# A tuned attention and gated feed-forward kernel: six tiles' x summed in PSUM, the flag inside the plan, another order at a chunk's end

## The chip, the cores and the metric

The kernel runs on one core of a Trainium2 chip. The metric is the device time of one execution in microseconds (us); for the kernel before it was taken three times, and a fourth execution was profiled. All rows and times below come from these runs. The engines are called as the profile calls them: PE (TensorE), DVE (VectorE), ACT (ScalarE), POOL (GpSimd) and SP (SyncE, which issues the transfers).

## The reference

```python
# attention: q, k, v are (4, 8, 768, 64), n_sink = 4, window = 128
scores = q @ k.transpose(0, 1, 3, 2) / sqrt(64)
keep = (pos_k < n_sink) | ((pos_q - pos_k >= 0) & (pos_q - pos_k < window))
a = softmax(where(keep, scores, -1e9))
x = (a @ v).transpose(0, 2, 1, 3).reshape(3072, 512)
# gated feed-forward on the 3072 tokens, d_model 512, d_ff 1536
out = (1 / (1 + exp(-(x @ w_gate))) * (x @ w_val)) @ w_out
```

Everything is fp32. The matrix products of the second part are made from split halves: each operand is a rounded "high" part and the rest as a "low" part, and a product is high x high + high x low + low x high.

## The kernel before, in words

**Attention.** A tile is 128 queries of one batch; tiles are worked in twelve pairs, heads by twos, so `attend` (L991) is called four times per pair of tiles, with a step number `u`. It makes the scores on PE (into the PSUM banks `a` or `o`), the masked exponential on DVE and ACT (`P`, `negm_all`, `sums`), turns P on PE (transposes `a<-ident,P`), copies it to `wt`, and multiplies it with v (`pv_one`, into a bank `a`); ACT copies that product into the SBUF buffer `xr` (256 columns for two heads). After the last heads of a pair `join` (L1260) adds the four sink keys: their probabilities `psk` are turned, copied to `sk`, multiplied with `vsp` into another bank, and DVE adds the bank to `xr`, 512 columns at a time. Then `copy` makes the high half `XH<-xr`, and `rest` the low half `XL<-xr,XH` (POOL or DVE).

There are four PSUM banks `a`, two `o` and two `m`. Scores, transposes, products with v and sink products share the banks `a`.

**Feed-forward.** Four of the twelve pairs (0, 1, 2 and 4) feed "direct" chunks while attention goes on: up products `m<-XH,wgh` and so on into the banks `m`, which DVE (`traw<-traw,m`) and ACT empty into `traw` and `graw`, and down products `o<-woh,graw`. The weights come in compressed and are decoded on the way (`w<-wst,zs`, then a high part `woh<-w` on ACT and its rest `wol<-w,woh` on DVE or POOL). The other eight pairs are stored to DRAM and come back later as four "wino" chunks: a Strassen-like form with seven products in place of eight (`passing` and `staying`, L2006 onward). A passing product has a rotating bank, which ACT or DVE adds to a sum `tf` in SBUF; three of the sums stay in banks `o` and `a`. At a chunk's end `merge` combines the sums with four additions and `emit` makes and stores four pieces of the output. In the kernel before all of that hangs behind the chunk's seventh product:

```python
fourth = coming.pop()
def done():
    fourth()
    merge(ci, sums)
    for n in range(4):
        emit(ci, g, n, O[n] if n < 3 else None, sums[n], False)
coming.append(done)
```

**The order.** No scheduler on the chip decides anything: a planner in Python (`Plan`) takes all operations with priorities, several possible engines and estimated lengths, and writes one fixed sequence per engine, with one helper line (L677 in the kernel before). Tables `RANKS` with hand-set numbers shift priorities of single operations. Where the planner sees PE without work in the first stretch it puts in filler matmuls `m<-ident` (`warm`), which compute nothing that is used.

**The end.** After the plan, DVE works out whether the inputs leave the fast path's limits (`bad`, five short instructions), PE sums that over the partitions (`a<-bad,one`), DVE makes `flag` and `total`, and every engine loads `total` and branches past the general path.

Of the kernel before, what the change touches and what calls it, by code (L numbers as in the profile page):

```python
# [9 lines left out]
F32 = mybir.dt.float32  # L10
# [12 lines left out]
NS = 4  # L23
# [8 lines left out]
RING = 6  # L32
# [47 lines left out]
SPLIT = 6  # L80
B_xr = 3
# [17 lines left out]
    A={0: 3.311, 10: -0.027, 200: 0.565, 400: -0.264, 600: -1.393, 635: 1.038, 665: -0.494, 695:  # L99
# [13 lines left out]
    G={0: 0.185, 200: -0.659, 400: -0.409, 600: 0.225, 635: -0.824, 665: 0.44, 695: -0.702, 725:  # L113
# [13 lines left out]
    M={0: -0.075, 2: -0.117, 3: -0.01, 4: 0.249, 5: -0.142, 6: -0.593, 7: -0.005, 8: 0.004, 9:  # L127
# [11 lines left out]
    P={0: 1.715, 200: 0.337, 400: -2.664, 600: 0.068, 1200: 0.132, 1500: -0.09, 1600: 2.607,  # L139
# [481 lines left out]
def kernel(  # L621
# [185 lines left out]
    for i in range(len(OS)):  # L807
        plan.over[f"o{i}", 0] = {("eO", i)}
# [1535 lines left out]
```

## Time and profile before

| what | us |
|---|---|
| runs | 714.39, 716.55, 717.35 |
| median | 716.55 |
| profiled execution, own time | 718.86 |
| its span, first to last instruction | 717.1 |
| mean granted TensorE clock (1 is full) | 0.996 |
| busy: PE / DVE / ACT / POOL | 700.7 / 570.0 / 381.4 / 522.2 |

The profiled execution is 718.86 − 716.55 = 2.31 us above the median of the runs, and 718.86 − 717.1 = 1.76 us of it lie outside the span. Busy time is a share of the span by engine; for PE the ends of matmuls are modelled. What an engine waits for in front of an instruction stands in brackets behind it, in us, with the releaser.

### The profile page before, as it was taken

The numbers are of one execution on the slowest core, as the hardware profiler recorded it, in microseconds if no ns is written. First come the engines' busy times: TensorE is split into PE (matmuls) and PEld (weight loads), VectorE is DVE, ScalarE is ACT, GpSimd is POOL, SyncE is SP. The second block draws the span as 40 slices with busy tenths as digits, with TensorE's granted clock in tenths as the row PEclk, the third lists the DMA queues.
The fourth block names the chain that finished last, engine by engine and source line by source line (L and its number), as shares of the span: only waits on it lengthen the run. The fifth ranks groups of instructions, "written<-read, shape, count | busy, mean of one in ns | idle before, by whom it ended". The sixth has DMA issues, their size and how long they took to land.

```text
span 717.1 us, 18023 instructions
## 1 busy us (share of the span) xinstructions
PE 700.7 (98%) x6488; PEld 649.7 (91%) x6488; DVE 570.0 (79%) x1296; ACT 381.4 (53%) x1052; POOL 522.2 (73%) x490
## 2 busy tenths in 40 slices
PE   8999899999999999999999999999899999999997
PEld 7778788888887888888999999999899999999996
DVE  8999989989895677875567798668888688886765
ACT  6898867754544565652453454543445444454431
POOL 3889867699997877764477697775768687786651
PEclk9999999999999999999999999999999999999999
DMA  9987879667776888855757656666467756665611
GB/s 291 295 245 257 289 235 311 233 211 251 245 246 193 273 264 264 283 143 173 233 178 227 185 163 202 210 220 186 154 182 216 227 184 176 184 206 183 187 50 64
DMA packets 110609, 152.75 MB, mean 213 GB/s; under 512 B 11060, under 2 KB 69428, under 8 KB 110516
## 3 DMA queue, kind: packets, MB, share of 16 engines
q1 hardware_dynamic: 110512, 151.56, 67.4%
q8 instruction: 52, 0.85, 0.5%
q14 instruction: 41, 0.34, 0.1%
q10 hardware_dynamic: 4, 0.00, 0.0%
HBM read 124.26 MB, written 27.26 MB: 211 GB/s over the span
## 4 chain that ended last, share of the span: by engine, by line
PE 77%; DVE 12%; DMA 4%; issue 3%; ACT 2%; POOL 1%; SPq 0%; DVEq 0%; POOLq 0%; ACTq 0%
PE a L677 38%; PE m L677 24%; PE o L677 15%; DVE tf L677 3%; DMA out_dram<-tf 2%; DVE w L677 2%; DVE a L677 1%; DVE tt L677 1%; DVE P L677 1%; DVE traw L677 1%; DMA wst<-in_moe_w_gate_dram 1%; DMA wst<-wol_d 1%; DVE XH L677 1%; DMA tf<-tw_d 1%; ACT P L677 1%
## 5 line engine op out<-in xcount | busy, mean ns | idle before, releaser
L677 POOL TENSOR_TENSOR tt<-tf,tt 128x512 fp32r<-128x512 f32 x75 | 103.3, 1389 | 26.9 <-ACT tt L677 11.6
L677 ACT ACTIVATE P<-P,negm_all 128x132 f32<-128x132 f32 x176 | 70.0, 399 | 23.7 <-DVE negm_all L677 23.4
L677 POOL TENSOR_SCALAR_AFFINE_SELECT wt<-wt 128x512 f32<-128x512 f32 (+1 forms) x88 | 63.1, 719 | 15.6 <-ACT wt L677 12.4
L677 PE MATMUL o<-woh,graw 128*128 128x512 f32 x192 | 74.1, 410 | 0.2 <-DVE graw L677 0.2
L677 ACT ACTIVATE tf<-a 128x512 f32<-128x512 f32 x49 | 29.3, 599 | 84.3 <-DVE a L677 62.3
L677 PE MATMUL m<-XH,wvh 128*128 128x256 f32 x216 | 61.6, 296 | 0.9 <-ACT traw L677 0.5
L677 ACT CAST tt<-tf 128x512 fp32r<-128x512 f32 x72 | 44.6, 620 | 27.9 <-PE a L677 21.8
L677 PE MATMUL m<-XH,wgh 128*128 128x256 f32 x193 | 56.5, 293 | 2.1 <-DVE traw L677 2.1
L677 PE MATMUL a<-xa,tt 128*128 128x256 f32 x360 | 57.2, 281 | 0.2 <-DVE a L677 0.2
L677 PE MATMUL m<-XH,wvl 128*128 128x256 f32 x204 | 57.4, 281 | 0.0
L677 PE MATMUL m<-XL,wvh 128*128 128x256 f32 x204 | 57.4, 281 | 0.0
L677 PE MATMUL m<-XH,wgl 128*128 128x256 f32 x192 | 54.4, 283 | 0.0
L677 PE MATMUL m<-XL,wgh 128*128 128x256 f32 x192 | 54.3, 283 | 0.0
L677 POOL TENSOR_TENSOR XH<-tf,XH 128x512 fp32r<-128x512 f32 x25 | 34.1, 1364 | 24.0 <-ACT XH L677 21.6
L677 PEld LDWEIGHTS a<-xa,tt 128*128 128x128 f32 x360 | 49.3, 188 | 0.5 <-DVE a L677 0.4
L677 POOL TENSOR_TENSOR XL<-tf,XL 128x512 fp32r<-128x512 f32 x14 | 18.2, 1303 | 41.2 <-ACT XL L677 41.2
L677 POOL TENSOR_TENSOR P<-P,rs 128x528 f32<-128x528 f32 x34 | 42.7, 1256 | 7.1 <-DVE rs L677 2.4
L677 PEld LDWEIGHTS m<-XH,wvh 128*128 128x128 f32 x216 | 40.0, 189 | 7.0 <-issue 2.9
L677 PEld LDWEIGHTS o<-woh,graw 128*128 128x128 f32 x192 | 36.1, 188 | 10.6 <-issue 3.7
L677 DVE TENSOR_TENSOR a<-a,big 128x256 f32<-128x256 f32 x72 | 30.4, 425 | 18.3 <-PE a L677 17.1
L677 PEld LDWEIGHTS m<-XH,wgh 128*128 128x128 f32 x193 | 36.7, 190 | 6.7 <-DVE traw L677 2.9
L677 DVE COPY_PREDICATED a<-tri,a 128x256 f32<-128x256 int32 (+1 forms) x90 | 30.7, 377 | 13.6 <-PE a L677 13.6
(409 smaller groups left out, 2647.1 us busy)
## 6 DMA issues: line engine op xcount, KB each, us to landing
tf<-tw_d SPq DMA_DIRECT2D x96, 256.0 KB, 3.2
wol<-wol_d SPq DMA_DIRECT2D x90, 256.0 KB, 3.5
qkT<-in_k_dram SPq DMA_DIRECT2D x30, 198.0 KB, 4.1
wgh<-tu_d SPq DMA_DIRECT2D x46, 128.0 KB, 2.7
wgl<-tu_d SPq DMA_DIRECT2D x46, 128.0 KB, 2.9
wvh<-tu_d SPq DMA_DIRECT2D x46, 128.0 KB, 2.6
wvl<-tu_d SPq DMA_DIRECT2D x46, 128.0 KB, 3.5
v<-in_v_dram SPq DMA_DIRECT2D x30, 192.0 KB, 3.6
```

The source lines that it names most:

```text
L677: return lambda *a, **kw: tc.keep_in_program_order(op(*a, **kw))
```

## The change

Four things change. First, for the first three pairs (`DIRECT = 3`; six tiles, the first twelve calls of `attend`) the products with v of the four head pairs write into two banks, each over 512 columns, and stay there; the sink products are added into the same banks, and the halves are made from there by the new function `straight`. The high half is made by ACT or DVE, the low half by DVE alone. Second, the flag's eight instructions are operations of the plan, at the end of attention. Third, the order of the seven products of the three wino chunks before the last is 0, 1, 2, 3, 5, 4, 6, and the pieces are stored as each is ready. Fourth, all numbers in `RANKS` are others (some 800; only their first line is shown), so that every engine's sequence is another one.

```diff
+DIRECT = 3
+HOLD = 1500.0
+OUTP = 0.5
...
-    A={0: 3.311, 10: -0.027, 200: 0.565, 400: -0.264, 600: -1.393, 635: 1.038, 665: -0.494, 695:
...
+    A={0: -0.166, 10: -8.671, 200: -1.192, 600: -1.977, 605: 0.724, 635: 1.407, 695: 0.285, 700:
...
+    for i in (1, 2):
+        plan.over["m2", i] = {("eM", 0)}
...
+        direct = n_of[b, t0] < DIRECT
         if h % 4 == 0:
-            XS.append(Tile(XR_, None, F32, "xr", 3))
+            if not direct:
+                XS.append(Tile(XR_, None, F32, "xr", 3))
+            elif u == 0:
+                XS.append(Tile(MS[1:], None, F32, "eM", 1))
+            else:
+                XS.append(Tile(AS, None, F32, "a", len(AS)))
...
         sides = [Tile(AS, None, F32, "a", len(AS)) for _ in range(2 - one)]
+        if direct:
+            assert one and T == 2 and not place[b, t0][0]
+            sides = [xst]
...
+        home = c * W if direct else 0
...
-                        sides[0]()[e * D : e * D + D, c0 : c0 + n], lhsT=vt()[:, e, l],
+                        sides[0]()[e * D : e * D + D, home + c0 : home + c0 + n], lhsT=vt()[:, e, l],
...
-                        start=i == 0, stop=i == len(wide) - 1, skip_group_check=True,
+                        start=i == 0 and not home, stop=i == len(wide) - 1, skip_group_check=True,
...
-            plan.op(
-                u, [("A", act(W, True), lambda: A.copy(out=xs()[:, c], in_=sides[0]()[:, 0:W]))],
-                [sides[0]], [(xst, c)],
-            )
+            if not direct:
+                plan.op(
+                    u, [("A", act(W, True), lambda: A.copy(out=xs()[:, c], in_=sides[0]()[:, 0:W]))],
+                    [sides[0]], [(xst, c)],
+                )
...
+    def straight(u, g, T, XS, sk, runs):
...
+        for i, acc in enumerate(XS):
+
+            def add(i=i, acc=acc):
+                for c in range(2):
+                    PE.matmul(
+                        acc()[:, c * W : c * W + W], lhsT=vs()[:, 2 * i + c], rhs=sk(),
+                        start=False, stop=True, skip_group_check=True,
+                    )
...
+            plan.op(
+                u, [
+                    ("A", act(2 * W, True), lambda x=x, hi=hi: A.copy(out=hi(), in_=x())),
+                    ("V", vec(2 * W), lambda x=x, hi=hi: V.tensor_copy(out=hi(), in_=x())),
+                ], [acc], [(XH, p) for p in parts],
+            )
+            rest(u, 2 * W, lo, x, hi, [acc] + [(XH, p) for p in parts], [(XL, p) for p in parts], True)
...
+        if n_of[b, t0] < DIRECT:
+            straight(u, g, T, XS, sk, runs)
+            return
...
-            fourth = coming.pop()
...
+            out_of = lambda n: lambda: emit(ci, g, n, O[n] if n < 3 else None, sums[n], False)
+            order = (0, 1, 2, 3, 5, 4, 6)
+            coming[:] = [coming[x] for x in order]
+            also(2, out_of(0))
+            also(4, lambda: merge(ci, sums), out_of(3))
+            also(5, out_of(2))
+            also(6, out_of(1))
...
+    plan.op(B * NT * H // 2 + 1.0, [("V", 900, odd_values)], [NEGM], [FLAG])
+    plan.op(B * NT * H // 2 + 1.0, [("PE", 200, counted)], [FLAG], [count])
+    plan.op(B * NT * H // 2 + 1.0, [("V", 400, decided)], [count], [FLAG])
```

The built programs count as follows, before and after: ACT copies `xr<-a` of 256 columns 48 and 36; DVE additions `xr<-a,xr` of 512 columns 22 and 18; the two `xr<-o,xr` are gone; `XH<-xr` on ACT 8 and 2, and three `XH<-a` and one `XH<-m` on ACT and two `XH<-a` on DVE are new; `XL<-xr,XH` on POOL 6 and 1, on DVE 2 and 1, and five `XL<-a,XH` and one `XL<-m,XH` on DVE are new. From the new numbers: fillers 50 and 45 (each is two matmul passes in the profile); `P<-P,rs` on POOL 34 and 25, on DVE 10 and 19; the rests of decoded weights on DVE 16 and 9, on POOL 20 and 27; `tt<-tf,tt` on POOL 75 and 67, on DVE 21 and 29.

Three places where the sequences differ. The first is DVE in the second pair of tiles, around the up product whose bank `m` is emptied by `traw<-traw,m`. `w<-wst,zs` and `wol<-w,woh` are the decoding of weights, `rs`, `a<-tri,a` and `P` belong to attention. Before:

```order
L677 SCALAR_TENSOR_TENSOR w_1358<-wst_1097,zs_121 128x512 [waits DMAHW7_49]
L677 CAST vsp<-w_1263 96x512 [waits DMAHW2_49]
L677 TENSOR_TENSOR wol_1398<-w_1358,woh_174 128x512 [waits DMAHW1_49,Activation_49]
L677 TENSOR_REDUCE rs_1406<-sums_126 128x4
L677 RECIPROCAL rs_1406<-rs_1406 128x4 [waits DVE_49]
L677 COPY_PREDICATED a_94<-tri,a_94 128x2x128 [waits PE_49]
L677 COPY_PREDICATED a_93<-tri,a_93 128x2x128 [waits PE_49]
L677 ISA P_1419,negm_all<-a_94,am_119 128x132 [waits DVE_49,Pool_49]
L677 ISA negm_all 128x1
L677 SCALAR_TENSOR_TENSOR traw<-traw,m_132 128x256 [waits PE_49]
```

And in the changed kernel, where the bank of the fourth group of gate weights is emptied:

```order
L683 SCALAR_TENSOR_TENSOR w_1303<-wst_1208,zs_122 128x512 [waits DMAHW5_49,Pool_49]
L683 SCALAR_TENSOR_TENSOR traw<-traw,m_133 128x256 [waits PE_49]
L683 TENSOR_REDUCE rs_1323<-sums_126 128x4 [waits Activation_49]
L683 RECIPROCAL rs_1323<-rs_1323 128x4 [waits DVE_49]
L683 CAST graw<-traw 128x256
L683 TENSOR_TENSOR wgl_177<-w_1303,wgh_176 128x512 [waits Activation_49]
L683 TENSOR_TENSOR vsp<-w_1265,vsp 32x512 [waits DMAHW3_49,Activation_49]
L683 COPY_PREDICATED a_96<-tri,a_96 128x2x128 [waits PE_49]
L683 COPY_PREDICATED a_95<-tri,a_95 128x2x128 [waits PE_49]
```

Before, the rest `wol<-w,woh`, two short and two masking instructions and a pass over the scores stand between the decode step and the emptying of the bank; now the emptying stands right behind the decode step, and no rest of 512 columns stands ahead of it there. (The rest of the group that stood here, `wol` of group 6, is now in POOL's sequence.)

The second place is ACT behind the end of the first wino chunk, where the first sums `tf` of the next chunk are written: these buffers hold the pieces that are being stored. A wait on a DMAHW semaphore is one for a transfer. Before:

```order
L677 ACTIVATE tf3_5350<-m0_131 128x512 [waits PE_49]
L677 ACTIVATE tf0_5226<-a2_95 128x512 [waits DVE_49,Activation_49]
L677 CAST XL_89<-tf0_5226 128x2x256 [waits DVE_49]
L677 ACTIVATE tf1_5254<-a0_93 128x512 [waits PE_49,Activation_49]
L677 ACTIVATE tf9_5445<-o0_97 128x512 [waits DMAHW4_49]
L677 CAST tt0_4943<-tf8_4895 128x512 [waits DMAHW3_49,PE_49]
L677 ACTIVATE tf5_5394<-o1_98 128x512 [waits DMAHW5_49,Pool_49]
L677 CAST wvh9_0_1885<-tf1_5254 128x256 [waits DVE_49]
L677 ACTIVATE tf4_5360<-o0_97 128x512 [waits DMAHW0_49,PE_49]
```

And in the changed kernel:

```order
L683 ACTIVATE tf3_5341<-m0_132 128x512 [waits PE_49]
L683 ACTIVATE tf0_5214<-a2_95 128x512 [waits DVE_49]
L683 CAST XL_89<-tf0_5214 128x2x256 [waits DVE_49]
L683 ACTIVATE tf5_5385<-m0_132 128x512 [waits DMAHW0_49,PE_49]
L683 ACTIVATE tf1_5244<-a0_93 128x512 [waits PE_49,Pool_49]
L683 CAST tt2_5034<-tf6_5038 128x512 [waits DMAHW5_49,PE_49,Pool_49]
L683 CAST wvh9_0_1670<-tf1_5244 128x256 [waits DVE_49]
L683 ACTIVATE tf4_5351<-o0_97 128x512 [waits DMAHW2_49,PE_49]
```

`tf9<-o0` has left this engine: it stands on DVE now. `tf5` and `tf4` still wait for transfers that read their buffers.

The third place is SP's sequence. At its end before:

```order
L677 DMA out_0_dram<-tf3_5350 128x2x256 [waits DMAHW0_49,DVE_49]
L677 DMA out_0_dram<-tf4_5360 128x2x256 [waits DVE_49]
L677 DMA out_0_dram<-tf9_5445 128x2x256 [waits DMAHW2_49,DVE_49]
L677 DMA out_0_dram<-tf5_5394 128x256 [waits DMAHW3_49,DVE_49]
L677 DMA out_0_dram<-tf5_5394 128x256 [waits DMAHW4_49,DVE_49]
L2287 TENSOR_LOAD total_9500 [waits DVE_49]
L2287 ISA x2
```

In the changed kernel, at row 331 of some 750, among the transfers of the last attention steps:

```order
L683 DMA xw_d_136<-xr_92 128x512 [waits DMAHW0_49,DVE_49]
L683 DMA v1_4842<-in_v_dram 128x2x192 [waits PE_49]
L683 DMA tf7_4877<-tw_d_137 128x512 [waits DMAHW2_49,PE_49,Activation_49]
L2359 TENSOR_LOAD total_189 [waits DVE_49]
L2359 ISA x2
L683 DMA wol1_4909<-wol_d_139 128x512 [waits DMAHW3_49,PE_49]
L683 DMA xw_d_136<-xr_92 128x512 [waits DMAHW4_49,DVE_49]
```

SP's load of `total` stood behind the last store; it now stands in the middle, and the transfers behind it there wait for it. On the other four engines the load of `total` stays the last step.

## Rows read from the trace of the kernel before

**Rows 1.** Page, part 1: busy time, share of the span, instructions
```profile
PE 700.7 (98%) x6488; PEld 649.7 (91%) x6488; DVE 570.0 (79%) x1296; ACT 381.4 (53%) x1052; POOL 522.2 (73%) x490
```

**Rows 2.** PE's waits: us in total, how often, the longest
```profile
PE m L677 <- DVE traw L677: 2.1, 2, 1.9
...
PE o L677 <- DVE tf L677: 1.7, 2, 1.0
PE a L677 <- DVE one L677: 1.5, 1, 1.5
PE o L677 <- ACT tf L677: 1.3, 2, 1.1
PE m L677 <- DVE tf L677: 1.0, 2, 0.6
...
PE a L677 <- ACT xr L677: 0.5, 2, 0.3
...
PE m L677 <- ACT tf L677: 0.3, 1, 0.3
```

**Rows 3.** Windows: stretch, length, busy us of PE, PEld, DVE, ACT, POOL
```profile
70.00:80.00 10.00, 10.00 (x103) 7.99 (x103) 9.63 (x28) 8.40 (x27) 9.63 (x9) 1.00 0.84 255
80.00:90.00 10.00, 8.14 (x74) 6.55 (x73) 9.12 (x35) 8.43 (x29) 7.09 (x10) 0.97 0.93 311
510.00:520.00 10.00, 8.08 (x65) 7.48 (x64) 10.00 (x15) 4.10 (x8) 7.16 (x6) 1.00 0.45 144
```

**Rows 4.** Timeline of PE, 86 to 89 us: start, length, instruction
```profile
86.34 0.60 PE L677 MATMUL a<-ident,P 128*128 128x128 f32 x4
88.80 0.39 PE L677 MATMUL m<-XH,wgh 128*128 128x256 f32 x1 [1.86 <-DVE traw L677]
```

**Rows 5.** Timeline of DVE, 85 to 89 us
```profile
85.41 1.73 DVE L677 TENSOR_TENSOR wol<-w,woh 128x512 fp32r<-128x512 f32 x1 [0.35 <-ACT woh L677]
...
88.33 0.42 DVE L677 SCALAR_TENSOR_TENSOR traw<-traw,m 128x256 f32<-128x256 f32 x1
```

**Rows 6.** Windows; granted clock behind POOL's busy time
```profile
87.50:90.00 2.50, 1.20 (x8) 1.20 (x9) 2.44 (x12) 1.96 (x8) 1.80 (x3) 0.90 1.03 374
90.00:92.50 2.50, 2.50 (x22) 1.71 (x21) 1.22 (x2) 1.72 (x7) 1.68 (x3) 0.50 0.48 119
92.50:95.00 2.50, 2.50 (x23) 2.33 (x20) 2.13 (x10) 1.20 (x6) 0.79 (x2) 0.92 0.79 259
```

**Rows 7.** Groups of ACT, DVE, POOL: count, busy us, mean ns
```profile
L677 ACT COPY xr<-a 128x256 f32<-128x256 f32 x48 | 17.7, 369 | 10.7 <-PE a L677 10.6
...
L677 DVE TENSOR_TENSOR xr<-a,xr 128x512 f32<-128x512 f32 x22 | 15.0, 682 | 2.3 <-PE a L677 2.1
L677 DVE TENSOR_TENSOR tt<-tf,tt 128x512 fp32r<-128x512 f32 x21 | 27.4, 1306 | 4.8 <-ACT tt L677 4.3
...
L677 POOL TENSOR_TENSOR wvl<-w,wvh 128x512 fp32r<-128x512 f32 x8 | 11.8, 1480 | 3.3 <-ACT wvh L677 3.3
...
L677 POOL TENSOR_TENSOR XL<-xr,XH 128x512 fp32r<-128x512 f32 x6 | 9.7, 1620 | 0.0
```

**Rows 8.** Timeline of PE, fillers in the head
```profile
16.02 2.05 PE L677 MATMUL m<-ident 128*128 128x128 f32 x16
```

**Rows 9.** Timeline of ACT and PE behind a chunk's end
```profile
459.09 0.60 ACT L677 ACTIVATE tf<-o 128x512 f32<-128x512 f32 x1 [1.86 <-DMA out_dram<-tf]
...
459.74 0.38 PE L677 MATMUL o<-wvh,XL 128*128 128x256 f32 x1 [1.08 <-ACT tf L677]
```

**Rows 10.** Timeline of all engines at the end
```profile
711.54 0.28 PE L677 MATMUL o<-woh,XL 128*128 128x256 f32 x1
711.86 0.76 DVE L677 SCALAR_TENSOR_TENSOR tf<-o,tf 128x256 f32<-128x256 f32 x2 [0.73 <-PE o L677]
...
713.31 0.19 PE L677 MATMUL a<-bad,one 128*1 128x4 f32 x2 [1.49 <-DVE one L677]
...
713.72 0.14 DVE L677 TENSOR_REDUCE total<-flag 1x1 int32<-1x4 int32 x1
```

More of the change, by code (lines that the diff above doesn't have):

```diff
@@ L775 @@
     READY, ready = Fixed(None), iter(range(1000))
+    NEGM, FLAG = Fixed(None), Fixed(None)
     AS = [ps.tile([128, 512], F32, name=f"a{i}") for i in range(B_a)]
@@ L815 @@
     val = keep.tile([128, 2], F32, name="val")
+    bad = keep.tile([128, 4], F32, name="bad")
     nsk, win = val[:, 0:1], val[:, 1:2]
@@ L949 @@
     ))])
+    cleared = []
     for i in range(len(OS) + BUFS["a"]):
@@ L958 @@
         ], w=[x])
+        cleared.append(x)
+    plan.op(SCALP, [("G", 60, lambda: G.memset(bad[:, 3:4], 0.0))], cleared)
     plan.op(SCALP, [("V", 530, scalars)], w=[nums])
@@ L969 @@
     place, home_of, n = {}, ([], []), 0
+    n_of = {}
     for b in range(B):
@@ L974 @@
             place[b, t0] = n in SPILL, len(to)
+            n_of[b, t0] = n
             to += range(b * NT + t0, b * NT + t0 + T)
@@ L1101, in attend @@
                     [sc[e]] + [(MASKS, x) for x in ((0,), (1, 4), (2, 4))[min(t0 + t, 2)]],
-                    [(P, (e, t))],
+                    [(P, (e, t)), (NEGM, (u, e, t))],
                 )
@@ L1240, in rear @@
                 )],
-                [vt, wt] + list(r), sides + [(xst, c)] + list(w), parts=True,
+                [vt, wt] + list(r), sides + [(xst, c)] * (not direct) + list(w), parts=True,
             )
-            plan.op(
-                u, [("A", act(W, True), lambda: A.copy(out=xs()[:, c], in_=sides[0]()[:, 0:W]))],
-                [sides[0]], [(xst, c)],
-            )
+            if not direct:
[3 more added lines that the diff above has]
+                )
             if not one:
@@ L1258, in attend @@
         return rear
+    def straight(u, g, T, XS, sk, runs):
+        W, vs = T * 128, VSP
+        assert runs == [[0, 1]]
+        k = g % RING * 128
+        for i, acc in enumerate(XS):
[5 more added lines that the diff above has]
+                    )
+            plan.op(u, [("PE", 2 * mac(W), add)], [vs, sk], [acc])
+            x = lambda acc=acc: acc().rearrange("p (c x) -> p c x", c=2)
+            hi, lo = (lambda i=i, z=z: z()[:, 2 * i : 2 * i + 2, k : k + W] for z in (XH, XL))
+            parts = [(2 * i + c, (g + t) % RING) for t in range(T) for c in range(2)]
+            plan.op(
[5 more added lines that the diff above has]
+            rest(u, 2 * W, lo, x, hi, [acc] + [(XH, p) for p in parts], [(XL, p) for p in parts], True)
     def join(u, b, t0, T, XS, psk):
@@ L2135, in downs, with also, made @@
         if p == NP - 1:
-            fourth = coming.pop()
-            def done():
-                fourth()
-                merge(ci, sums)
-                for n in range(4):
-                    emit(ci, g, n, O[n] if n < 3 else None, sums[n], False)
-            coming.append(done)
+            def also(n, *then):
+                product = coming[n]
+                def made():
+                    product()
+                    for x in then:
+                        x()
+                coming[n] = made
+            out_of = lambda n: lambda: emit(ci, g, n, O[n] if n < 3 else None, sums[n], False)
[5 more added lines that the diff above has]
+            also(6, out_of(1))
     def merge(ci, sums):
-        pr = -1000.0 + ci + 1 - 0.5 / NP
+        pr = -1000.0 + ci + 1 - OUTP / NP
         last = ci == len(MT) + WT - 1
@@ L2159, in emit @@
     def emit(ci, g, n, bank, acc, last):
-        pr = -1000.0 + ci + 1 - 0.5 / NP
+        pr = -1000.0 + ci + 1 - OUTP / NP
         r = home_of[1][g + n // 2 * 2] * 128
@@ L2188, in emit @@
                 in_=ot()[:, 0:512].rearrange("p (j d) -> p j d", j=2),
-            ), [ot],
+            ), [ot], slack=HOLD,
         )
@@ L2250, with odd_values, counted, decided @@
         feeds()
+    one = keep.tile([128, 1], F32, name="one")
+    nc.vector.memset(one, 1.0)
+    flag = keep.tile([1, 4], I32, name="flag")
+    total = keep.tile([1, 1], I32, name="total")
+    count = Tile(AS, None, F32, "a", len(AS))
+    def odd_values():
+        V.tensor_reduce(out=bad[:, 0:1], in_=negm_all, axis=AX.X, op=ALU.max)
+        V.tensor_scalar(
+            out=bad[:, 0:1], in0=bad[:, 0:1], scalar1=1.0e8, scalar2=None, op0=ALU.is_gt
+        )
+        for i, (x, y, op) in enumerate(
+            ((win, 1.0, ALU.is_lt), (win, float(WIN), ALU.is_gt), (nsk, float(NS), ALU.is_gt))
+        ):
+            V.tensor_scalar(out=bad[:, i + 1 : i + 2], in0=x, scalar1=y, scalar2=None, op0=op)
+    def counted():
+        PE.matmul(count()[0:1, 0:4], lhsT=one, rhs=bad, start=True, stop=True)
+    def decided():
+        V.tensor_copy(out=flag, in_=count()[0:1, 0:4])
+        V.tensor_reduce(out=total, in_=flag, axis=AX.X, op=ALU.max)
+    plan.op(B * NT * H // 2 + 1.0, [("V", 900, odd_values)], [NEGM], [FLAG])
+    plan.op(B * NT * H // 2 + 1.0, [("PE", 200, counted)], [FLAG], [count])
+    plan.op(B * NT * H // 2 + 1.0, [("V", 400, decided)], [count], [FLAG])
     ci = state["ci"]
@@ L2263 @@
     wres = {f: [w() if i < 4 else w()[:, 0] for i, w in enumerate(ws)] for f, ws in wres.items()}
-    bad = keep.tile([128, 4], F32, name="bad")
-    V.tensor_reduce(
-        out=bad[:, 0:1], in_=negm_all, axis=AX.X, op=ALU.max
-    )
-    V.tensor_scalar(
-        out=bad[:, 0:1], in0=bad[:, 0:1], scalar1=1.0e8, scalar2=None, op0=ALU.is_gt
-    )
-    for i, (s, x, op) in enumerate(
-        ((win, 1.0, ALU.is_lt), (win, float(WIN), ALU.is_gt), (nsk, float(NS), ALU.is_gt))
-    ):
-        V.tensor_scalar(out=bad[:, i + 1 : i + 2], in0=s, scalar1=x, scalar2=None, op0=op)
-    one = keep.tile([128, 1], F32, name="one")
-    V.memset(one, 1.0)
-    count = AS[0]
-    PE.matmul(count[0:1, 0:4], lhsT=one, rhs=bad, start=True, stop=True)
-    flag = keep.tile([1, 4], I32, name="flag")
-    V.tensor_copy(out=flag, in_=count[0:1, 0:4])
-    total = keep.tile([1, 1], I32, name="total")
-    V.tensor_reduce(out=total, in_=flag, axis=AX.X, op=ALU.max)
     main.close()
```

18 lines of the change are left out of this document (9 added, 9 removed), and 233 rows, old and new, of tables (A, G, M, P).

## The prediction

> **What bounds the kernel now.** I read first the page's busy times: PE is busy for 700.7 of 717.1 us, 98% [rows 1]. So a change can gain in three ways only: less work on PE, fewer of the 717.1 − 700.7 = 16.4 us in which PE stands, or less time at the span's ends. All that the other engines save is worth nothing unless PE waits for them. Second I read PE's list of waits [rows 2], which sorts these microseconds by releaser; the reader is to see that they are few and short, and that the largest is a single one, 1.9 us for a DVE `traw`. Third the windows, to see where the other engines have no slack: between 70 and 80 us PE, DVE and POOL are all busy for over 9.6 of 10 us, at 80 to 90 PE loses 1.9, and at 510 to 520 PE has 8.08 while DVE has 10.00 [rows 3]. Fourth, the timeline at the places that this shows: around 87 us [rows 4, 5], behind a wino chunk's end [rows 9] and at the end [rows 10].
>
> **The profiled execution and the runs.** All terms come from the profiled execution, whose own time is 718.86; the median of the runs is 716.55. I take the difference from the trace and set it off against the median. A change of 0.5%, 3.6 us, is about what a measurement of this kernel can tell from none: faster means under 712.97, slower over 720.13.
>
> **The end.** PE's last matmul that counts starts at 711.54; DVE's last additions run from 711.86 to 712.62. Then come `bad`, `one`, PE's sum at 713.31, `flag`, and `total` to 713.86 [rows 10]. With the flag in the plan the engines can load `total` and branch from 712.62 on, 713.86 − 712.62 = 1.24 us earlier. What follows, 717.1 − 713.86 = 3.2 us, stays. The last stores are issued beside this and could end later than the branch; bounds 0 and −1.2, value **−1.2**, since 3.2 us are left for them to land. The flag's own work now stands inside: PE's 0.19 us on the path, **+0.2**; DVE's part, 712.62 to 713.86 less PE's step, is at most 1.1 us at the end of attention, where DVE is not full on average [rows 1], bounds 0 and 1.1, value 0. PE's sum waits there for DVE's `bad`, and down products `o<-woh,graw` are queued behind it; but `bad` needs only the last pass over the scores, which the transposes ahead of the sum wait for by way of ACT anyway. SP's load of `total` moves ahead of weight loads and of stores of `xr`. It waits for DVE's `total`; behind it `wol` waits for PE work and `xr` for DVE work that stand later than `total` in their own sequences, so the load delays nothing that was ready: 0.
>
> **Fillers.** 45 instead of 50, each two passes; 16 passes take 2.05 us [rows 8], so 5 × 2 × 0.128 = 1.3 us less on PE. They stand where PE would wait in any case, so it may be nothing: bounds 0 and −1.3, value the middle, **−0.6**.
>
> **The stall at 87 us.** PE's four transposes start at 86.34, and the next up product starts at 88.80, after 1.86 us idle, released by `traw` [rows 4]. DVE has only just emptied the bank, at 88.33, because a `wol<-w,woh` of 1.73 us stood ahead from 85.41, and a reduction and masking behind that [rows 5]; the sequences in the section on the change show both. After the idle the granted clock falls: 0.90, 0.50 and 0.92 in three windows of 2.5 us, with 0.50 the lower of the two levels, 1.2 GHz [rows 6]. That costs (0.10 + 0.50 + 0.08) × 2.5 = 1.7 us of matmul time. So the stall costs 1.9 + 1.7 = 3.6 us. In the changed sequence the emptying of the bank follows straight behind the decode step, `wol` of group 6 is POOL's, and the ACT copies and sums of x that crowd this stretch are fewer. Bounds 0 and −3.6; I take all of it, **−3.6**, because what held the bank is gone from in front of it.
>
> **x in PSUM.** Removed: 12 ACT copies of 369 ns, 4.4 us; on DVE six additions of 0.68, 4.1 us; on POOL five `XL` of 1.62, 8.1 us [rows 7]. Added: on DVE six low halves from PSUM and one less from SBUF, and two high halves. No row shows either from PSUM; the nearest is `xr<-a,xr`, one PSUM operand and 512 columns, 682 ns, so 7 × 0.68 = 4.8 us. Were they all twice as slow (the `XL` on POOL is 1620), 9.5. DVE is thus about even, 0.7 worse, bounds 0 and 5.4 over some 100 us. All of it is hidden where PE is the bound; on the path only the wait for the banks counts. The two banks of a pair are held from its first product with v to its last half, so of four `a` banks one to three are gone in the second and third pair, and scores, transposes and sink products share the rest. What a missing bank costs has no row. Its lower bound is a gain: PE waits 0.5 us in all for `xr<-a` [rows 2], and those copies go. Its upper bound is one stall like that at 87 us, +3.6. Nearest are the small waits of the list, 0.3 to 0.6 each, so I take one more of the larger kind, **+0.5**.
>
> Against this part stands a rule of the Trainium skill, "Perfetto Trace Analysis", section Matmuls: independent groups of matmuls should go round the PSUM banks, so that one is emptied by ACT or DVE while the next is written, and an accumulation group keeps its one bank. By that rule alone the accumulators take away places to turn to, and the sum would be nearer to the last rival's 722.0 than to mine. No run here has yet shown a held bank.
>
> **A chunk's end.** At 459.09 ACT can write the next chunk's `tf` only after 1.86 us of waiting for a store out of it, and PE stands for 1.08 us behind ACT [rows 9]. All of PE's waits for ACT's `tf` come to 1.3 + 0.3 = 1.6 us [rows 2]. With the new order the first piece is ready after the third product instead of the seventh, two after the fifth and sixth, so three of four stores can go some products earlier. Bounds 0 and −1.6. ACT's waits for transfers remain in the sequence, but for stores that were issued earlier, and one of the writes goes to DVE. Value **−1.6**.
>
> **More rests on DVE later.** `tt<-tf,tt` on DVE goes from 21 to 29, 8 × 1.306 = 10.4 us [rows 7], in the wino stage, where DVE's average slack is wide but 510 to 520 has none [rows 3]. There PE's waits for DVE's `tf` are now 1.7 + 1.0 = 2.7 us [rows 2]. Bounds 0 and a doubling, +2.7; nearer to the low end, because DVE has a fifth of the span free: **+1.0**.
>
> **Sum.** −1.2 + 0.2 − 0.6 − 3.6 + 0.5 − 1.6 + 1.0 = −5.3. Profiled execution 718.86 − 5.3 = 713.6, median 716.55 − 5.3 = **711.2**.
>
> **Rivals.**
>
> *The stall stays, by POOL.* The rests taken from DVE go to POOL: decode rests there go from 20 to 27, 7 × 1.48 = 10.4 us more, while five `XL` and nine `P` normalisations leave it. Between 70 and 80 us POOL already has 9.63 of 10 [rows 3]. An up product that waits for a decoded low part on POOL, or for DVE's normalisations that came over, would stop PE as `traw` did, and the clock falls with it. For it: POOL is fuller than DVE there. Against it: the low parts are made well ahead. Without the 3.6 us: 711.2 + 3.6 = 714.8.
>
> *DVE becomes the limit in the wino stage.* If of the 10.4 us on DVE somewhat under half (4.7) comes out on PE instead of 1.0: 711.2 + 3.7 = 714.9. For it speaks 510 to 520 us, against it the mean of 79%.
>
> *All hides.* No new waits, the larger DVE load is hidden, and DVE's `tf` waits go with the earlier chunk end: 711.2 − 0.5 − 1.0 − 2.7 = 707.0. For it: PE's waits there come from single late instructions, which another order may place well.
>
> *The held banks.* Slower. With one to three of four banks `a` held, scores cannot be written ahead of the transposes of the step before, so PE stops at a pair's border until the halves are made, and each stop costs the idle time and the clock, 3.6 us as at 87 us. With the stall at 87 not gone and two more: 711.2 + 3 × 3.6 = 722.0. Two in all give 718.4, still no change; from three on it decides. For it: four banks serve three kinds of groups, and DVE, which empties them, is busy for 9.63 of 10 [rows 3]. Against it: the products with v no longer take a bank of their own per step, nor the sink products one.
>
> **Chances and range.** Forecast 0.46, held banks 0.10, stall by POOL 0.20, DVE in the wino stage 0.12, all hides 0.12. Faster is forecast and all hides, 0.58; same is the two middle rivals, 0.32; slower 0.10. The range goes from just under the best rival, 706.0, to two stalls' 718.4, rounded 718.5; outside lie the held banks and a little below, under 0.2. The bounds of the unknown terms lie inside: with every one at its better end the sum gains a further 0.6 + 1.0 + 1.0 = 2.6, with the stall at its worse end it loses 3.6. The forecast's own range is 709 to 713.
>
> **What would show it.** Right: no PE wait over 1 us around 87 us and a clock of 1.00 through 80 to 100; ACT's waits for `out_dram` behind the chunks gone and PE's for ACT `tf` near 0; the span ending about 3.2 us after DVE's last `tf`; filler passes 90; ACT's `xr<-a` x36. Wrong: waits of PE for a bank `a` or for `XH` and `XL` at 25 to 110 us with the clock under 1; more than 3.7 us of PE waits for DVE's `tf` after 400 us; PE's wait for POOL's low parts; stores that land after the branch. The forecast is wrong as a whole if PE's busy time, now 700.7, moves by more than the fillers and the clock explain, for then something other than waits changed.

## The result and the profile after

The changed kernel takes 710.84 us (median of five runs, 709.55 to 711.29), the kernel before 716.55 (714.39 to 717.35): ratio 0.9909, 95% interval 0.9887 to 0.993, so 5.7 us or 0.9% faster. Run again beside other kernels it took 710.37 against 715.84 (0.9929, 0.9904 to 0.9955). Forecast were 711.2 and a range of 706.0 to 718.5.

The profiled execution of the changed kernel took 709.55 with a span of 707.8; that is 9.3 us under the span of the profile before, more than the medians differ. Its page has, against [rows 1]:

```profile
span 707.8 us, 17961 instructions
...
PE 694.5 (98%) x6478; PEld 645.4 (91%) x6478; DVE 571.4 (81%) x1305; ACT 373.3 (53%) x1033; POOL 521.1 (74%) x483
```

PE is still busy for 98%. Against [rows 2], PE's list of waits (us in total, how often, the longest):

```profile
PE m L683 <- POOL ident masks.py:199: 1.8, 1, 1.8
PE a L683 <- ACT xr L683: 1.6, 2, 1.0
PE a L683 <- POOL tt L683: 1.4, 2, 1.2
PE a L683 <- DVE rs L683: 0.6, 1, 0.6
...
PE m L683 <- DVE tf L683: 0.3, 1, 0.3
```

The waits for `traw` of 1.9, for ACT's `tf` and for DVE's `one` are gone, DVE's `tf` is down from 2.7 to 0.3. What has grown is ACT's copies `xr`, from 0.5 to 1.6, in pairs that still make them; new are 0.6 for `rs` on DVE at 91 us and 1.4 for rests `tt` on POOL. The windows that answer to [rows 3]:

```profile
80.00:90.00 10.00, 10.00 (x96) 8.17 (x94) 9.81 (x30) 6.97 (x26) 7.07 (x9) 1.00 0.89 287
510.00:520.00 10.00, 10.00 (x86) 10.00 (x86) 8.45 (x12) 5.95 (x13) 10.00 (x7) 1.00 0.62 185
```

PE is full in both. In the second, DVE has come down from 10.00 to 8.45, and POOL is now the full one; but the kernels are over 5 us apart by then, so the same 10 us hold other work. The halves from PSUM, for which the trace before had no row:

```profile
L683 DVE TENSOR_TENSOR XL<-a,XH 128x512 fp32r<-128x512 f32 x5 | 3.2, 680 | 0.0
...
L683 DVE CAST XH<-a 128x512 fp32r<-128x512 f32 x2 | 1.4, 682 | 0.0
```

They cost 680 and 682 ns, the 682 that were taken from `xr<-a,xr` [rows 7].

A profiled execution is one draw. So each kernel below is read by three marks of its profiled execution: where the last down product of the direct chunks starts (the stage with attention ends there), where the last product of all starts, and the span's end.

| kernel | direct ends | products end | span | wino stage | behind it |
|---|---|---|---|---|---|
| before, first profile | 347.3 | 711.5 | 717.1 | 364.2 | 5.6 |
| before, again | 344.9 | 706.9 | 712.5 | 362.0 | 5.6 |
| before, first transfers in the new order | 345.1 | 707.9 | 713.5 | 362.7 | 5.6 |
| before, one rest later | 346.6 | 708.6 | 714.2 | 362.0 | 5.6 |
| changed, first profile | 341.7 | 702.2 | 707.8 | 360.6 | 5.6 |
| changed, again | 342.5 | 702.4 | 707.5 | 359.9 | 5.1 |
| changed, first transfers in the old order | 342.6 | 702.4 | 708.5 | 359.7 | 6.1 |
| changed, flag at the end | 341.5 | 700.9 | 706.5 | 359.4 | 5.6 |
| changed, old chunk end | 342.4 | 705.2 | 710.8 | 362.8 | 5.7 |
| changed, without the branch | 344.7 | 706.9 | 710.8 | 362.1 | 4.0 |

Single profiles of one sequence differ by nearly as much as the kernels do: the first of the kernel before is its slowest by 2.9 us, and of the changed kernel's the one without the branch has the latest last product; both hold stalls that the others lack (below). With all rows taken, the first stage ends on average at 346.0 before and 342.6 after, 3.4 us earlier, the wino stage (five rows of the new chunk end) takes 360.3 instead of 362.7, 2.4 us less, and what is behind it is 5.6 both times where the branch stands. That is 5.8 us, against 5.7 between the medians.

### The profile page after: what moved, and what is told of

It is laid out like the page before. It is cut to its first block, busy times and chain, and to the rows that moved or that the text cites. A ratio compares the mean times of both kernels' runs of the same rounds, so it can differ in the third digit from the quotient of the medians.

```text
span 707.8 us, 17961 instructions
## 1 busy us (share of the span) xinstructions
PE 694.5 (98%) x6478; PEld 645.4 (91%) x6478; DVE 571.4 (81%) x1305; ACT 373.3 (53%) x1033; POOL 521.1 (74%) x483
## 4 chain that ended last, share of the span: by engine, by line
## 5 line engine op out<-in xcount | busy, mean ns | idle before, releaser
L683 POOL TENSOR_TENSOR tt<-tf,tt 128x512 fp32r<-128x512 f32 x67 | 94.5, 1422 | 25.8 <-ACT tt L683 17.6
L683 POOL TENSOR_SCALAR_AFFINE_SELECT wt<-wt 128x512 f32<-128x512 f32 (+1 forms) x88 | 68.1, 775 | 9.7 <-ACT wt L683 6.7
L683 POOL TENSOR_TENSOR XH<-tf,XH 128x512 fp32r<-128x512 f32 x27 | 38.0, 1408 | 22.2 <-ACT XH L683 21.4
L683 POOL TENSOR_TENSOR XL<-tf,XL 128x512 fp32r<-128x512 f32 x15 | 19.7, 1313 | 42.7 <-ACT XL L683 33.5
L683 DVE TENSOR_TENSOR tt<-tf,tt 128x512 fp32r<-128x512 f32 x29 | 37.0, 1276 | 5.5 <-ACT tt L683 4.6
L683 DVE CUSTOM_DVE_ANT_0 P<-a,am 128x132 f32<-128x132 f32 x164 | 40.5, 285 | 0.1
```

What stands on the lines that cost most here:

```text
L683: return lambda *a, **kw: tc.keep_in_program_order(op(*a, **kw))
```

## The experiments

In all of them the order of instructions is the planner's, and where an edit says "order", the finished list was edited before it was issued, so that everything else stands where it stood (only buffer numbers in names change). Kernels that were run together share their runs of the kernel before, and ratios are against these.

**The changed kernel again.** No edit.

> The changed kernel unaltered, as the measure for the other runs of this call. Expected: 710.8 us, with the profiled execution within 2 us of it. If the 1.2 us of the end were real and only one late store hid them in the profile shown, the span behind PE's last product is 4.0 to 4.3 us here; if not, about 5.3 again.

Measured: 710.37 us, profiled execution 709.2. The span ends 5.1 us after the last product starts. That is between the two expectations: 0.5 us of the tail's 1.2 may have come in this execution, and none in the first.

**The flag back at the end.**

```diff
+    plan.at_end = (odd_values, counted, decided)
...
+        last = [x for x in order if x[2] in self.at_end]
+        order = [x for x in order if x[2] not in self.at_end] + last
         for o, e, fn in order:
```

> The changed kernel with the flag's eight instructions taken out of the plan's order and issued behind its last step, as in the kernel before; everything else stands in the same order. Theory of the prediction (moving the flag is worth 1.2 us at the end and costs 0.2 inside): 1.0 us slower than the changed kernel, 711.8, and 1.2 us more between PE's last product and the span's end. Rival, from the changed kernel's trace (5.3 us from PE's last product to the end, as before): the last stores' landing has taken the flag's place as what ends last, so the time stays within 0.3 us of 710.8.

Measured: 709.65 us, ratio 0.9916 (0.989 to 0.9942), beside 0.9929 for the changed kernel: not slower, and by the medians 0.7 us faster, which is inside both intervals. The move of the flag gave nothing that shows. The timeline of the changed kernel's end (PE and DVE) shows that the compute part of the term was right; [rows 10] is the counterpart:

```profile
702.22 0.28 PE L683 MATMUL m<-woh,XL 128*128 128x256 f32 x1
702.53 0.76 DVE L683 SCALAR_TENSOR_TENSOR tf<-m,tf 128x256 f32<-128x256 f32 x2 [0.73 <-PE m L683]
```

DVE is done at 703.29, and no flag follows. But the span ends at 707.8, 4.5 us later, not 3.2. Its transfers in that window (queue, how many, KB each, us from issue to landing):

```profile
out_dram<-tf SPq DMA_DIRECT2D x2, 256.0 KB, 4.1
out_dram<-tf SPq DMA_DIRECT2D x2, 128.0 KB, 2.9
```

And in the kernel with the flag at the end, the same four stores:

```profile
out_dram<-tf SPq DMA_DIRECT2D x2, 256.0 KB, 2.2
out_dram<-tf SPq DMA_DIRECT2D x2, 128.0 KB, 1.8
```

With the flag in the plan the last stores take 4.1 and 2.9 us instead of 2.2 and 1.8: they have become what ends last. In the changed kernel's first profile, its second and the one with the first transfers in the old order the stores of 256 KB took 4.1, 3.5 and 4.3 us, and the span ended 5.6, 5.1 and 6.1 us behind the last product, in the same order.

**No branch.** The changed kernel without the load of `total`, the branch and the general path behind it, which is left out here.

```diff
-    tc.mark_branch_hint_location("rare", "LikelyTaken", engines=mybir.ALL_ENGINES)
-    flagged = nc.values_load(total[0:1, 0:1], min_val=0, max_val=512)
-    with tc.If(flagged > 0, label="rare"):
-        general(tc, q, k, v, ident, nsk, win, wres, wol_d, out)
```

> The changed kernel without the load of total, the branch and the general path behind it (which these inputs never take); the flag's arithmetic stays. Theory (with the flag in the plan the early branches' instruction fetches run among the last stores and delay their landing by 0.5 to 1.4 us, which eats the 1.0 us that the move should bring): the last store lands 2.3 to 2.4 us behind PE's last product, as in the kernel before, and the span ends 4.3 us or less behind it; 709.5 or less. Rival (the stores land late for a reason of the stores' own order): landing 2.8 us or more behind PE's last product again.

Measured: 709.61 us. The stores, in its transfers at the end:

```profile
out_dram<-tf SPq DMA_DIRECT2D x2, 256.0 KB, 2.2
out_dram<-tf SPq DMA_DIRECT2D x2, 128.0 KB, 1.7
```

The landing is back at 2.2 and 1.7 us, and the span ends 4.0 us after the last product starts, so the theory holds for the stores: with `total` known early, each engine can take its branch as soon as it is done, and what the branch brings with it runs among the last stores and delays them. In the whole time that can't be seen: the six runs lie between 706.75 and 712.89. That it is the fetch of instructions in particular is the likeliest reading (the transfers of the changed kernel's last 7 us hold three packets of the instruction queues, and these stand among the stores instead of behind them), but only the branch as a whole was taken away.

This profile is the slowest of the six runs, and it holds two stalls that the other profiles of the changed kernel have shorter or not at all, though the sequences ahead of the end are the same. PE's list of waits begins with

```profile
PE o L683 <- DMA wol<-wol_d: 2.1, 1, 2.1
PE a L683 <- POOL tt L683: 1.9, 1, 1.9
```

and behind them, from 120 and from 610 us on, the clock falls to about the lower level, 1.2 GHz:

```profile
120.00:122.50 2.50, 2.50 (x10) 2.00 (x8) 1.60 (x11) 0.87 (x2) 0.48 (x2) 0.51 0.88 291
612.50:615.00 2.50, 2.50 (x14) 2.50 (x14) 1.46 (x3) 0.65 (x2) 1.67 (x2) 0.50 0.09 34
```

**The old chunk end in the changed kernel.** `also(...)` and the new order of products are replaced by the old `done()`, and `HOLD` by 0; up to the end of the first wino chunk the sequences are the same, behind it the planner deals them anew.

```diff
-            order = (0, 1, 2, 3, 5, 4, 6)
-            coming[:] = [coming[x] for x in order]
-            also(2, out_of(0))
-            also(4, lambda: merge(ci, sums), out_of(3))
-            also(5, out_of(2))
-            also(6, out_of(1))
+            fourth = coming.pop()
+            def done():
+                fourth()
+                merge(ci, sums)
+                for n in range(4):
+                    emit(ci, g, n, O[n] if n < 3 else None, sums[n], False)
+            coming.append(done)
```

> The changed kernel with the old chunk end: products in the old order, all additions and stores behind the seventh, no slack on the stores; up to the end of the first wino chunk the sequences are the same as in the changed kernel. Theory (PE's waits behind ACT's and DVE's tf at the chunk ends come from stores that start late, and the new order removes them): PE's waits for tf rise from 0.3 to 2 to 4 us, ACT's waits of 1.5 us and more for out_dram come back at three places, the time is 1.6 to 4 us longer, 712.4 to 714.8. Rival (the waits were an accident of where the old numbers put the stores; the new numbers would avoid them with either chunk end): under 0.7 us longer, 711.5 at most.

Measured: 713.54 us (712.11 to 715.31), ratio 0.9964 (0.9948 to 0.998), 3.2 us slower than the changed kernel. ACT's waits for the stores are back; its list of waits has

```profile
ACT tf L683 <- DMA out_dram<-tf: 3.8, 6, 1.2
```

as in the second profile of the kernel before:

```profile
ACT tf L677 <- DMA out_dram<-tf: 2.5, 5, 0.6
```

In the changed kernel there is no such row; there the two groups of ACT that waited for stores before, `tf<-m` and `tf<-o` (count, busy, mean ns, idle before and its releasers), wait for PE alone:

```profile
L683 ACT ACTIVATE tf<-m 128x512 f32<-128x512 f32 x6 | 3.6, 598 | 0.8 <-PE m L683 0.7
L683 ACT ACTIVATE tf<-o 128x512 f32<-128x512 f32 x6 | 3.6, 596 | 2.3 <-PE o L683 2.3
```

PE's waits for `tf` rise from 0.3 us (0.8 in the second profile) to 2.0, the low end of what was expected. More of the 3.2 us is in the wino stage's busy time, as the two windows of the wino stage show, first the changed kernel (again), both stages, then the one with the old chunk end:

```profile
0.00:342.50 342.50, 335.09 (x3471) 288.06 (x3472) 287.59 (x919) 207.30 (x697) 265.66 (x289) 1.00 0.78 249
342.50:702.70 360.20, 358.35 (x3008) 356.41 (x3006) 280.77 (x384) 166.97 (x337) 254.80 (x194) 1.00 0.61 186
```

```profile
342.40:705.40 363.00, 360.01 (x3008) 357.03 (x3006) 281.13 (x384) 164.91 (x335) 256.82 (x196) 1.00 0.60 185
```

Of 2.8 us between the two second stages (360.2 and 363.0), 1.1 are idle (1.85 and 2.99) and 1.7 are busy time of the same 3008 matmuls. What makes the same matmuls longer was not tested; a first product behind a wait is listed with 0.38 us [rows 9], one in a run with 0.28 [rows 10].

**One rest later in the kernel before.** The rest `wol<-w,woh` that stood ahead of the emptying of the bank at 87 us, and its store, are issued behind that emptying.

```diff
+        late = [order[620], order[628]]
+        order = order[:620] + order[621:628] + order[629:634] + late + order[634:]
         for o, e, fn in order:
```

> The kernel before with one rest, the wol<-w,woh that stood ahead of the emptying of the bank at 87 us, issued behind that emptying (its store to DRAM follows it); all else as before. Theory (this rest alone made the stall of 1.9 us, and the stall made the clock fall for 1.7 us): the wait at 87 us is under 0.3 us, the clock stays full through 100 us, the time is 3 to 3.6 us shorter, 713.0 to 713.5. Rival (DVE and POOL are full there, so another late instruction stops PE a little later): the wait moves or halves, the clock may still fall, and less than 1.2 us is gained, over 715.3.

Measured: 717.52 us, ratio 1.0018 (1.0001 to 1.0035). The stall is gone, with the clock at 1.00, but its time is not gained; windows as in [rows 6]:

```profile
87.50:90.00 2.50, 2.42 (x26) 2.04 (x26) 2.33 (x9) 1.08 (x4) 0.83 (x1) 1.00 0.75 266
95.00:97.50 2.50, 1.52 (x8) 0.84 (x7) 2.42 (x6) 2.02 (x7) 2.14 (x3) 1.00 0.58 165
```

At 95 to 97.5 PE loses 1.0 us to a `traw` on ACT and an `sk`. Both theories were half right, and the time said that something was wrong with the premise, so the kernel before was profiled again.

**The kernel before again.** No edit.

> The kernel before unaltered, profiled once more, because taking away the rest ahead of the 87-us stall removed the stall and left the time where it was. Theory (the stall and the clock drop at 87 us belong to every execution): PE waits 1.5 us or more for traw near 87 us and the clock is 0.5 for a few us behind it, in a span of about 716. Rival (they were chance in the one execution shown, which was 2.3 us above the median): no wait over 0.5 us there, full clock through 80 to 100 us, a span of 713 to 715.

Measured: 716.16 us, profiled execution 714.25 with a span of 712.5. The windows in which the first profile had the stall and the clock at 0.50 [rows 6], and the one before them:

```profile
85.00:87.50 2.50, 2.50 (x23) 2.18 (x24) 2.40 (x9) 1.89 (x5) 2.36 (x3) 1.00 1.06 351
87.50:90.00 2.50, 2.42 (x28) 2.03 (x29) 2.47 (x9) 2.42 (x10) 2.42 (x4) 1.00 1.03 367
90.00:92.50 2.50, 2.50 (x31) 2.19 (x23) 2.15 (x9) 2.06 (x7) 1.96 (x5) 1.00 1.00 344
```

No stall, full clock; PE's largest wait for `traw` is 0.8 us, at 63 us. Nor is it in the profile of the next experiment, whose sequences there are the same. It was chance in the one execution shown. The rest of 1.73 us in [rows 5] shows how: here the same instruction takes

```profile
85.56 0.68 DVE L677 TENSOR_TENSOR wol<-w,woh 128x512 fp32r<-128x512 f32 x1
```

and POOL's sum `vsp` starts behind it, as it does in the next experiment:

```profile
86.38 1.30 POOL L677 TENSOR_TENSOR vsp<-w,vsp 32x512 fp32r<-32x512 f32 x1
```

In the first profile that sum had started first, 0.12 us ahead of the rest:

```profile
85.29 1.30 POOL L677 TENSOR_TENSOR vsp<-w,vsp 32x512 fp32r<-32x512 f32 x1 [0.51 <-DVE vsp L677]
```

The rest ended 0.55 us after it. That the one held up the other fits these rows (spans on POOL are rough), but was not tested.

**The first seven transfers.** SP's first seven transfers stand in another order in the changed kernel (q, k, v ahead of the first packed weight). Each kernel was given the other's.

```diff
+        slots_ = (1, 5, 9, 12, 14, 17, 21)
+        first = [order[x] for x in (5, 12, 17, 1, 9, 14, 21)]  # in the changed kernel (12, 1, 14, 5, 17, 9, 21)
+        for x, y in zip(slots_, first):
+            order[x] = y
```

> The kernel before with SP's first seven transfers in the order of the changed kernel: q, k and v of the first step, then the packed weight, then the second step's k, q and v; all else as before. Theory (the changed kernel's head is 1.5 to 3 us shorter in idle time and slow clock, because the first scores do not wait behind a weight load of 512 KB-class size): 1.5 us or more shorter, under 714.5. Rival (the head's differences are luck of single executions): within 0.7 us of the kernel before.

> The changed kernel with SP's first seven transfers in the order of the kernel before, the packed weight first and the two steps' k, q, v taking turns; all else as in the changed kernel. Theory of the head: 1.5 to 2.5 us longer, 712.0 to 713.0. Rival: within 0.7 us of 710.4, and what the changed kernel gains before 350 us comes from the sequences behind the head.

Measured: 715.64 us in the kernel before (1.0004, 0.9983 to 1.0026) and 710.16 in the changed one (0.9921, 0.9893 to 0.9949). The order of the first transfers is worth nothing that these runs can tell. In the profiles of this study the start differs from one execution to the next by more than that: PE's wait there for a transfer of q is 2.40 us, 1.31 us, or none.

**No pair in PSUM, new tables.**

```diff
-DIRECT = 3
+DIRECT = 0
```

> The changed kernel with no pair summed in PSUM (x goes through ACT's copies and xr in all pairs), with the flag in the plan, the new chunk end and the new tables; the tables were made for the other form, so the order of the first 110 us is dealt anew. Theory (x in PSUM frees ACT, DVE and POOL in the crowded first 100 us, and that is most of the gain before 350 us): 3 us or more longer than the changed kernel, over 713.5, with PE's waits before 130 us at 3 us or more. Rival (the new tables alone make the gain): within 1 us of 710.4.

Measured: 719.01 us, ratio 1.0048 (1.0028 to 1.0067), 8.6 us slower than the changed kernel. The direct stage ends at 347.9 instead of 342.5, and PE waits above all for what empties the banks `m`:

```profile
PE m L683 <- ACT traw L683: 3.3, 6, 1.3
...
PE m L683 <- DVE traw L683: 0.9, 2, 0.6
```

Only one of the six waits for ACT, 0.45 us at 47 us, lies in the stretch of the six tiles; the others lie between 135 and 284 us. The planner dealt the whole order anew, so this is the price of the new tables with the other form, and not of the copies and additions alone.

**The PSUM form with the old tables and the old chunk end** (the flag in the plan, since it comes with the same code).

```diff
-RANKS = dict(   # the new tables
+RANKS = dict(   # the old tables
...
-            order = (0, 1, 2, 3, 5, 4, 6)
+            fourth = coming.pop()
```

> The kernel before (its tables and its chunk end) with x of the first three pairs summed in PSUM and the flag in the plan; the planner deals the order anew from these tables. Theory (the PSUM form frees engines by itself, and the tables only follow it): 1 to 4 us faster than the kernel before, 712 to 715. Rival (held banks stop PE unless the order is made for them; the tables carry the gain): not faster, 716 or more, with waits of PE for banks or halves in the first 130 us.

Measured: 717.51 us, ratio 1.001 (0.9993 to 1.0028): nothing gained. Its direct stage ends at 347.8. PE's list of waits is led by

```profile
PE m L680 <- ACT traw L680: 2.7, 5, 0.9
PE a L680 <- DMA eq<-in_q_dram: 2.1, 1, 2.1
```

and no wait in it is for a held bank's halves. Here too the order was dealt anew. So neither the PSUM form nor the tables do it alone: each with the other's partner is no faster than before, or slower, and together the first stage is about 3 us shorter. What the form does in an otherwise equal order no run shows.

**Fillers.** The kernel before without its last five fillers (ten passes at about 32 us), and the changed kernel without any.

```diff
+        fills = [i for i, x in enumerate(order) if x[0] is None]
+        order = [x for i, x in enumerate(order) if i not in fills[-5:]]
...
+        order = [x for x in order if x[0] is not None]
```

> The kernel before without its last five fillers, ten passes at about 26 to 28 us, all else in the same order. Theory (fillers are PE work on the path, 1.3 us for five): the end of the direct chunks comes 1.0 to 1.3 us earlier than in the profiles of the kernel before, the time is 714.5 to 715. Rival (they fill waits that stay): the waits at that place grow by what the fillers leave, and the time is within 0.4 us of the kernel before.

> The changed kernel without any filler, all else in the same order. Theory (fillers buy the full clock early and cost nothing, since PE waits there for data): the clock rises later than 11 us, every step of the first 30 us is later, 1 to 4 us slower, 711.5 to 714.5. Rival (PE is not waiting for data there and the fillers only delay it): up to 3 us faster, 707.5 to 710, with the clock rising at most 3 us later.

Without the five: 719.70 us, ratio 1.0052 (1.0034 to 1.0069), 3.3 us slower, against both theories. The two stages tell where; the kernel before (again) first, then the one without the five:

```profile
0.00:344.90 344.90, 337.24 (x3479) 290.17 (x3480) 288.54 (x905) 214.36 (x713) 266.02 (x294) 1.00 0.77 247
344.90:707.20 362.30, 359.29 (x3008) 356.65 (x3006) 278.18 (x381) 167.39 (x340) 256.69 (x196) 1.00 0.60 185
```

```profile
0.00:343.60 343.60, 338.36 (x3469) 290.88 (x3470) 285.94 (x905) 214.47 (x713) 267.84 (x294) 1.00 0.77 248
343.60:711.50 367.90, 361.30 (x3008) 358.26 (x3006) 276.23 (x381) 167.06 (x340) 256.22 (x196) 1.00 0.59 182
```

The direct stage does end 1.3 us earlier here (between profiles of the kernel before its end varies by 2.4), although 0.6 us of new waits stand where the fillers were, but the wino stage takes 367.9 instead of 362.3 us. ACT waits there for the stores

```profile
ACT tf L679 <- DMA out_dram<-tf: 6.2, 6, 2.4
```

where it was 2.5 us in the second profile of the kernel before and 4.3 in the first, and behind the first chunk the clock falls:

```profile
455.00:457.50 2.50, 0.92 (x6) 0.78 (x6) 0.45 (x2) 1.57 (x4) 2.42 (x3) 1.00 0.63 195
457.50:460.00 2.50, 2.48 (x14) 2.41 (x14) 2.39 (x4) 1.44 (x4) 1.17 (x2) 0.62 0.42 141
```

Why the stores are waited for longer when all comes 1.3 us earlier is open; the longest run without the five is 721.7 and the shortest 718.1, so it is not one bad execution.

Without any filler the changed kernel takes 711.64 us (710.53 to 713.27), a ratio of 0.9922 (0.9903 to 0.9942) beside 0.9929 with them: the slowdown of 1 to 4 us that the theory expected does not show. The head does change. Windows of its head, and of the changed kernel's:

```profile
15.00:20.00 5.00, 2.49 (x22) 1.55 (x24) 4.63 (x9) 3.88 (x15) 4.93 (x6) 0.81 1.06 341
20.00:25.00 5.00, 5.00 (x40) 2.94 (x36) 4.11 (x13) 2.99 (x12) 4.69 (x8) 0.51 1.06 362
```

```profile
15.00:20.00 5.00, 4.68 (x47) 4.04 (x49) 3.65 (x9) 3.78 (x14) 4.93 (x7) 1.00 1.05 316
20.00:25.00 5.00, 4.71 (x62) 2.71 (x54) 4.94 (x18) 3.39 (x13) 4.79 (x7) 1.00 1.03 351
```

PE idles for half of 15 to 20 us and then works at 0.51 of the clock, where the filled head keeps 1.00. In the whole time that is not seen.

## Why the prediction was right, and where it was not

The time was right, 711.2 against 710.84, but in large part by luck. For the first stage the terms make −3.6 + 0.5 − 0.6 = −3.7, near the measured −3.4; yet the largest of them stands for something that the other profiles don't have, and what gave the 3.4 us was not priced. Then the end was taken 1.0 us too good and the wino stage 1.8 us too bad (−0.6 for −2.4), and these nearly cancel.

**The stall at 87 us (−3.6, "I take all of it").** Wrong. This was the step that failed: "I take the difference from the trace and set it off against the median." The stall and its clock drop belonged to one execution, which was 2.3 us above the median; two other profiles with the same sequence there don't have it, and a kernel that removes its cause runs no faster. The rows [rows 4, 5, 6] were read rightly, but for that execution alone. What the direct stage really gained is about 3 us (346.0 to 342.6 on average), 2.4 us between the two second profiles. Of these, 2.15 us are busy time of PE (337.24 to 335.09) and only 0.25 us idle time. Ten filler passes fewer are 1.3 us of the busy time. Which part of the change gave the rest is open.

**Fillers (−0.6).** Not settled. Where five fillers, 1.3 us of PE work, were taken out of the kernel before, 0.6 us of waits came in their place, but that kernel was 3.3 us slower; of the changed kernel without any no slowdown shows. No run has just the five that the change took.

**x in PSUM (+0.5).** The prices were right (680 against 682 ns), and no wait for a held bank stands in PE's lists: the rival of the held banks, and the bank rule of the Trainium skill on its side ("Perfetto Trace Analysis", section Matmuls), did not show in any profile. The rule asks that groups go round the banks so that emptying overlaps with filling; with two banks of four held and an order made for it the stage was shorter here (342.5 us), and with the old tables it was not (347.8). What the prediction missed is that form and tables belong together: it costed the form by itself, and with the old tables it gained nothing.

**A chunk's end (−1.6) and more rests on DVE (+1.0).** The first is right in the mechanism, but mis-sized: −3.2 by the experiment. ACT's waits for stores are there in every profile with the old chunk end, 2.5 to 6.2 us, and in none with the new one. The prediction counted only PE's waits for ACT's `tf`; with the stores go also PE's waits for DVE's `tf` (2.7 to 0.3) and busy time. For the second no experiment was made: the old chunk end leaves 28 of the 29 rests on DVE. Both together are −2.4 by the profiles, so that +0.8 would be left for the rests, less than single profiles differ.

**The end (−1.2 + 0.2).** Wrong. "3.2 us are left for them to land": they were not enough, because the early branch made the stores land later, 2.9 for 1.8 us. That was named as a bound of 0, and it is what happened; the span ends 4.5 us after DVE's last `tf`, where 3.2 was the sign of being right.

**The other rivals.** Behind the head PE waits for POOL only for `tt`, in the wino stage: 1.4 us in the first profile, 0.5 in the second, without a fall of the clock. In the profile without the branch it is 1.9 us, and the clock falls to 0.50 as that rival has it, only in another stage. DVE as the limit of the wino stage did not come.

**PE's busy time.** The prediction set a sign for being wrong as a whole: busy time that moves by more than fillers and clock explain. It moved from 700.7 to 694.5, and these explain 1.3 + 1.7 = 3.0 of the 6.2 us. The second profiles have 696.7 and 693.4 us, 3.3 less with no stall at 87 us in either, and fillers are 1.3 of it. So the sign came, and it is not explained in full. The rows show a part: the first product behind a wait is listed as longer, 0.38 or 0.39 us [rows 4, 9] for 0.28 [rows 10], with ends that are modelled. Busy time holds a part of what waits cost, and the idle 16.4 us were not all that an order could save.

**Sum.** −2.4 to −3.4 for the first stage, −2.4 to −3.2 for the wino stage, 0 at the end.

## What to carry to other kernels

Before a stall is priced, see it twice: a second profile of the same kernel here removed the largest term, and a later one of the changed kernel's sequences showed two stalls of chance of its own. Where a buffer is both a store's source and the next stage's target, the waits vary from run to run (2.5 to 4.3 us in four profiles of the kernel before and its small edits), and stores that start a few products earlier were worth more here than PE's waits for ACT in one trace. A table of hand-set priorities and the form of the work it was made for can't be priced one at a time.

## What was not expected of the hardware

- A branch that is decided early is not free at the end: the last stores took 2.2 and 1.8 us from issue to landing with the flag at the end, 3.5 to 4.3 and 2.3 to 3.0 with it in the plan, and 2.2 and 1.7 without the branch.
- The same DVE instruction can double: `wol<-w,woh` of 512 columns, both operands in SBUF, took 1.73 us in [rows 5] and 0.68 in the second profile of the same kernel, while `XL<-a,XH`, with one operand in PSUM, took 680 ns on average over five.
- Taking 1.3 us of filler out at 32 us made the kernel 3.3 us slower; in its profile the time is lost in waits some 420 us later.
